# A decode kernel's TensorE program put into one loop of six turns, with its loads re-ordered around it

## Chip, cores, metric

One core of a Trainium2 chip. The metric is the device time of one execution in microseconds, median over runs. Spans and instants are from one profiled execution of each kernel and count from its first instruction.

## The reference, cut to what matters

```python
xn = layernorm(x)                              # x: 2 x 1 x 448
q  = xn @ wq                                   # 448 x 4096: 16 heads of 256
k, v = last 2048 keys of each cache            # 2 x 8 heads x 2048 x 256 each
s  = softmax(q k^T / 16) v @ wo                # wo: 4096 x 448
g  = silu(relu(xn @ w1) @ w2)                  # 448 x 1792, 1792 x 448
out = x + s * g
```

One row per batch: nearly all of the work is reading 44.1 MB of K, V and weights from HBM. The caches are taken in four units u = (batch, half of the heads), each with 4.19 MB of K and 4.19 MB of V.

## The kernel before

A small helper writes one program per engine, with semaphores between them. SP issues all large loads in program order into one queue; PE (the matmul engine) runs the four units as a loop of four turns; DVE (VectorE) transposes K and does the softmax. What the argument needs (cuts marked with `# ...`):

```python
def load_k(u):      # two K buffers: k2 waits for the scores S(0), k3 for S(1)
    d_k[u] = pr.dma(SP, kbuf[u % 2][:, :], kv_src(u, A_k_cache), [st.get(("S", u - 2, NBLK - 1))])

def load_v(u, cuts=(0, NT)):     # v1 waits for PV(0), v2 for PV(1), v3 only for the q matmuls: own buffer
    deps = [None if u == 0 else st["q_mm"] if u == NU - 1 else st["PV", u - 1]]
    # ...

d_wq = [pr.dma(SP, wq_sb[:, 0:FIRST * HC], ...)]     # a part of wq
load_k(0)
d_wq.append(...)                                     # the rest of wq
load_k(1)
load_v(0)
st["w1"] = pr.dma(SP, w1_sb[:, 0:W2_AT], w1_src)
st["w2"] = pr.dma(SP, w2_sb[...], w2_src)
# ...
for blk in range(NBLK):
    do_T(0, blk)          # DVE: transposes of k0
do_q()                    # PE: 28 matmuls; DVE: q_n; PE: replicate; DVE: q_t
turn_q(0)                 # DVE: the masked q for unit 0
turn(0)                   # S(0), softmax
load_k(2)
turn(1)                   # T(1), S(1), PV(0), softmax, then h and F
load_v(1); load_k(3)
turn(2)
load_v(2); load_v(3, (0, 48, 64))
# ... seven parts of wo
turn(3)
# ... ten filler matmuls, PV(3), attend, wo in 9 tiled slots and 23 x 4 narrow matmuls
```

S(u) are the scores of unit u, T(u) the four transposes before it, PV(u) the weighted sum of V. "Attend" turns PV's result into columns for the wo matmuls, which the tile at_z holds. h is relu(xn @ w1), F is h @ w2, g its silu; xr is xn in columns. The "granted clock" is the share of its full clock that PE was given.

## Time and profile before

| | before |
|---|---|
| time, median (range) | 112.78 us (112.55 to 112.97), 4 runs |
| span of the profiled run | 109.8 us (a run of its own, of 111.31 us) |
| share of the span in which the 16 DMA engines are busy | 95% |
| busy share of PE, DVE | 55%, 57% |
| end of S(0), when k2 may be issued | 36.7 us |

### The profile page before, as it was taken

Reading aid. Unit: us, or ns where it says so; the run is one execution under the profiler, and the core shown is the slowest. Engines: PE = TensorE matmul, PEld = TensorE weight load, DVE = VectorE, ACT = ScalarE, POOL = GpSimd, SP = SyncE. Lnnn points to the kernel's source line nnn. Section 1 sums busy time; section 2 is a strip of 40 time slices with the busy share of each in tenths; the row PEclk is TensorE's granted clock in tenths of the full one; section 3 lists DMA queues with packets and bytes.
Section 4 is the critical chain, followed back from the end, with each engine's and each line's share of the span. In section 5 each row is a group of like instructions: output and inputs, shape, how many; then the busy total and the mean of one; then the engine's idle time right before and its main releaser. Section 6 shows DMA issues by size and latency. Waiting matters only on the chain. (4 is left out here: it accounts for less than half of the span.)

```text
span 109.8 us, 1368 instructions
## 1 busy us (share of the span) xinstructions
PE 60.4 (55%) x558; PEld 19.5 (18%) x558; DVE 63.0 (57%) x96; ACT 10.2 (9%) x19; POOL 3.1 (3%) x11
## 2 busy tenths in 40 slices
PE   0001000076599330899755597853039785898993
PEld 0000000020111020000241010112001011534792
DVE  0249109995400459993468999266299926624601
ACT  4990000000000110000200000020000002000000
POOL 7400000000000000000000000000000000000000
PEclk9999999999999995579996569997555899999999
DMA  3998989998899889998899999999999999899950
GB/s 60 502 388 382 549 371 395 439 537 382 382 453 501 382 367 416 411 548 382 382 501 394 406 406 465 441 406 406 465 441 406 444 430 430 361 419 410 402 207 7
DMA packets 3046, 44.15 MB, mean 402 GB/s; under 512 B 354, under 2 KB 612, under 8 KB 1508
## 3 DMA queue, kind: packets, MB, share of 16 engines
q1 hardware_dynamic: 3008, 44.11, 95.0%
q8 instruction: 2, 0.03, 0.1%
q10 hardware_dynamic: 36, 0.01, 0.1%
HBM read 44.11 MB, written 0.00 MB: 402 GB/s over the span
## 5 line engine op out<-in xcount | busy, mean ns | idle before, releaser
L379 DVE STREAM_TRANSPOSE kt<-kbuf 128x2048 f32<-128x2048 f32 x16 | 35.9, 2286 | 7.8 <-DMA kbuf<-in_A_k_cache_dram 7.8
L361 PE MATMUL sbk<-kt,qz 128*8 128x512 bf16 x128 | 31.1, 1073 | 13.6 <-PEq L102 13.5
L401 DVE TENSOR_REDUCE rm<-sbk 128x1 f32<-128x512 f32 x4 | 2.8, 692 | 14.6 <-PE sbk L361 14.6
L361 PE MATMUL obk<-vbuf,xr 128*4 128x512 bf16 x28 | 3.2, 626 | 13.9 <-DMA vbuf<-in_A_wq_dram 13.9
L407 ACT ACTIVATE et<-sbk,bias 128x512 bf16<-128x512 f32 x4 | 2.7, 687 | 81.1 <-DVE bias L405 81.1
L361 PEld LDWEIGHTS sbk<-kt,qz 128*8 128x8 bf16 x128 | 2.6, 87 | 28.9 <-issue 28.7
L361 PE MATMUL pbk<-et,spread 128*128 128x32 bf16 x64 | 2.6, 193 | 7.2 <-PEq L102 7.2
L361 PE MATMUL obk<-vbuf,pt 128*16 128x512 bf16 x96 | 5.8, 381 | 0.0
L361 PE MATMUL mbk<-ident,xg 2*128 2x2 bf16 x7 | 0.3, 163 | 8.5 <-DVE xg L325 8.5
L361 PE MATMUL wbk<-q_n,ident 128*128 128x512 bf16 x15 | 4.1, 395 | 1.4 <-DVE qz L396 1.4
L361 PE MATMUL hbk<-kbuf,at_z 128*8 128x112 bf16 x92 | 4.8, 213 | 0.0
L409 DVE STREAM_TRANSPOSE et<-et 128x512 bf16<-128x512 bf16 x4 | 2.8, 712 | 3.4 <-ACT et L407 3.4
L417 DVE TENSOR_TENSOR pt<-pbk,hmask 128x512 bf16<-128x512 f32 x4 | 2.8, 692 | 3.3 <-PE pbk L361 3.3
L361 PEld LDWEIGHTS hbk<-kbuf,at_z 128*8 128x8 bf16 x92 | 4.6, 87 | 0.1
L361 PEld LDWEIGHTS pbk<-et,spread 128*128 128x128 bf16 x64 | 2.2, 99 | 10.5 <-issue 10.5
L361 PEld LDWEIGHTS obk<-vbuf,pt 128*16 128x16 bf16 x96 | 2.5, 94 | 6.8 <-issue 4.7
L361 PEld LDWEIGHTS obk<-vbuf,xr 128*4 128x4 bf16 x28 | 0.8, 114 | 15.4 <-issue 15.4
L611 DVE TENSOR_TENSOR tmp<-hbk,g_sb 8x112 f32<-8x112 f32 x1 | 0.3, 262 | 4.4 <-PE hbk L361 4.4
L361 PE MATMUL fbk<-wf,h_z 128*2 128x448 bf16 x14 | 1.7, 567 | 1.7 <-DVE h_z L494 1.7
L456 DVE TENSOR_TENSOR at_exp<-mbk,qmask 128x128 bf16<-128x128 f32 x4 | 1.2, 292 | 2.5 <-PE mbk L361 2.5
L361 PE MATMUL obk_last<-vbuf,pt 128*16 128x512 bf16 x32 | 2.3, 380 | 0.0
L444 DVE TENSOR_SCALAR o_sb<-obk,rs 128x512 bf16<-128x512 f32 x3 | 2.2, 731 | 0.0
(80 smaller groups left out, 43.9 us busy)
## 6 DMA issues: line engine op xcount, KB each, us to landing
kbuf<-in_A_k_cache_dram SPq DMA_DIRECT2D x4, 4096.0 KB, 23.4
vbuf<-in_A_v_cache_dram SPq DMA_DIRECT2D x3, 4096.0 KB, 15.8
wf<-in_B_w_dram SPq DMA_DIRECT2D x2, 1568.0 KB, 42.4
vbuf<-in_A_v_cache_dram SPq DMA_DIRECT2D x1, 3072.0 KB, 22.5
vbuf<-in_A_wq_dram SPq DMA_DIRECT2D x1, 2560.0 KB, 20.9
vbuf<-in_A_wq_dram SPq DMA_DIRECT2D x1, 1024.0 KB, 6.1
vbuf<-in_A_v_cache_dram SPq DMA_DIRECT2D x1, 1024.0 KB, 24.4
kbuf<-in_A_wo_dram SPq DMA_DIRECT2D x1, 1008.0 KB, 26.2
```

What stands on the lines that cost most here:

```text
L361: return lambda e: e.matmul(out_ap, lhsT=lhsT, rhs=rhs, start=start, stop=stop, skip_group_check=True, **kw)
L379: st["kt", u, blk] = pr.op(DVE, lambda e: e.transpose(view(dst, 0, [[1, 32 * NT]]), view(src, 32 * blk, [[DH // 2, NT], [1, 32]])), [d_k[u ...
L401: v = pr.op(DVE, lambda e: e.tensor_reduce(out=rm[:, :], in_=sbk[:, :], axis=AX.X, op=ALU.max), [st["S", u, NBLK - 1]])
L407: a = st["exp", u] = pr.op(ACTE, lambda e: e.activation(e_sb, sbk[:, :], ACT.Exp, bias=bias[:, 0:1], accum_out=ssum[:, 0:1]), [v, st.get(( ...
L409: token = pr.op(DVE, lambda e: e.transpose(e_t, e_sb), [a, st.get(("Pt", u - 1))])
L417: st["pt", u] = pr.op(DVE, lambda e: e.tensor_tensor(out=view(pt, 0, [[8, NT], [2, 4], [1, 2]]), in0=view(pbk, 0, [[2, NT], [0, 4], [1, 2] ...
L444: st["osb", u] = pr.op(DVE, lambda e: e.tensor_scalar(out=o_sb[:, :], in0=view(out_bank(u), 0, [[1, 512]]), scalar1=rs[:, u:u + 1], scalar ...
L456: st["at", u] = pr.op(DVE, lambda e: e.tensor_tensor(out=view(at_exp, 0, [[16, 8], [8, 2], [1, 8]]), in0=view(mbk, 136, [[1, 8], [8, 2], [ ...
L611: v_t = pr.op(DVE, lambda e: e.tensor_tensor(out=tmp[:, :], in0=hbk[0:NROW, 0:NCOL], in1=g_sb[:, :], op=ALU.mult), [m_o, v_g])
```

## The change

Its intent is a smaller PE program: one loop of six turns with conditional parts, so that the last PV and both late attends need no code of their own; one V buffer, so that all PVs share code; h and xr by register loops; h computed before the loop, which needs w1 early; F and wo with fewer matmuls; two stores. Behind each of v0 to v2 SP now issues an almost empty transfer ("nil"), so that every PV can wait for two transfers, as PV(3) must for the two parts of v3. The core of the diff:

```diff
-            deps = [None if u == 0 else st["q_mm"] if u == NU - 1 else st["PV", u - 1]]
+            deps = [st["PV", u - 1] if u else None]
...
-        d_wq = [pr.dma(SP, wq_sb[:, 0:FIRST * HC], wq_src[:, 0:FIRST * HC])]
+        d_wq = pr.dma(SP, wq_sb[:, 0:SLOTS * HC], wq_src)
+        st["w1"] = pr.dma(SP, w1_sb[:, 0:W2_AT], w1_src)
         load_k(0)
-        d_wq.append(...)
         load_k(1)
         load_v(0)
-        st["w1"] = ...
-        st["w2"] = ...
...
         def do_H():
-            deps = [st["w1"]]
-            for s in range(SLOTS):
-                for i in range(4):
-                    ... 4 column tiles of 224
+            def body(e, s):
+                for j in range(7):
+                    o = mm(view(hbk, 64 + 4 * j, [[1, 4]]), view(w1_sb, FC * s + j, [[7, 128]]), view(xr, 4 * s, [[1, 4]]), False)(e)
+                return o
+            o = looped(SLOTS, body, [st["w1"]])
...
         for blk in range(NBLK):
             do_T(0, blk)
         do_q()
         turn_q(0)
-        idle_work(1, [st["q"]])
+        do_H()
+        pr.op(PE, None, [st["q"]])
         turn(0)
...
         load_v(2)
-        load_v(3, (0, 48, 64))
+        load_w2()
+        turn(3)
...     (first part of wo, then)
+                load_v(3)
...     (the other parts of wo)
-        idle_loop(5, 2)
-        ... PV(3), attend(2), attend(3) written out, filler matmuls
+        turn(NU)          # attend(2), F, PV(3)
+        turn(NU + 1)      # attend(3)
```

Attend moved from between the transposes to the head of each turn; F is 14 matmuls one after the other instead of four tiles side by side; wo is 16 tiled slots and 16 x 2 matmuls of 224 columns.

## The prediction

The "start-up ramp" is in the trace of the kernel before: 83, 181 and 385 GB/s in the second, third and fourth microsecond, 582 in the fifth. The doubling for strided reading was my estimate (0.08 us a pair from the 0.04 of the trace); the 0.5 us a turn and the 2 us restart of the rivals and the 1 us outside the span were suppositions, shown by no trace. That low PE use brings a low clock was not shown: the trace gives the clock of 0.57 and PE's busy time, 3.42 of 10 us, side by side from 74 to 84 us; the cold tail in the range was an estimate from that.

> **What bounds the kernel now.** I read the page first (engine shares, the slices, the DMA queue), then the waits of the DMA-issuing queue on SP, then the timeline. The page:
>
> ```profile
> DMA  3998989998899889998899999999999999899950
> ...
> q1 hardware_dynamic: 3008, 44.11, 95.0%
> ...
> HBM read 44.11 MB, written 0.00 MB: 402 GB/s over the span
> ```
>
> The sixteen DMA engines are busy from the second slice to the last but two; no compute engine passes 57%. The kernel is a stream of 44.1 MB with work hung beneath it. The timeline shows when SP issued the transfers, all in one queue:
>
> ```profile
> 5.10 1.09 SPq L42 DMA_DIRECT2D wf<-in_B_w_dram  x2
> 36.73 0.55 SPq L42 DMA_DIRECT2D kbuf<-in_A_k_cache_dram  x1
> 54.34 0.54 SPq L42 DMA_DIRECT2D vbuf<-in_A_v_cache_dram  x1
> 54.92 0.60 SPq L42 DMA_DIRECT2D kbuf<-in_A_k_cache_dram  x1
> 72.85 1.83 SPq L42 DMA_DIRECT2D vbuf<-in_A_v_cache_dram  x3
> ```
>
> and the waits of SP before them:
>
> ```profile
> SPq L42 <- PE obk L361: 34.4, 2, 17.3
> SPq L42 <- PE sbk L361: 30.5, 1, 30.5
> ```
>
> SP waits long, for PE to free K and V buffers, yet the DMA never pauses: what it issued earlier is still draining. So the quantity that decides is the lead, the time between the issue of a transfer and the moment the queue ahead of it would run dry. To get it I need landings. The waiting engines give them:
>
> ```profile
> 16.61 8.89 DVE L379 STREAM_TRANSPOSE kt<-kbuf 128x2048 f32<-128x2048 f32 x4 [5.30 <-DMA kbuf<-in_A_k_cache_dram]
> 22.78 3.16 PE L361 MATMUL obk<-vbuf,xr 128*4 128x512 bf16 x28 [13.91 <-DMA vbuf<-in_A_wq_dram]
> 25.99 0.69 DVE L478 TENSOR_SCALAR q_n<-obk 128x512 bf16<-128x512 f32 x1 [0.49 <-PE obk L361]
> 29.24 7.45 PE L361 MATMUL sbk<-kt,qz 128*8 128x512 bf16 x32
> 41.54 8.88 DVE L379 STREAM_TRANSPOSE kt<-kbuf 128x2048 f32<-128x2048 f32 x4
> 52.37 1.92 PE L361 MATMUL obk<-vbuf,pt 128*16 128x512 bf16 x32
> 59.51 2.31 DVE L379 STREAM_TRANSPOSE kt<-kbuf 128x2048 f32<-128x2048 f32 x1 [0.28 <-DMA kbuf<-in_A_k_cache_dram]
> 78.95 4.51 DVE L379 STREAM_TRANSPOSE kt<-kbuf 128x2048 f32<-128x2048 f32 x2 [2.27 <-DMA kbuf<-in_A_k_cache_dram]
> ```
>
> Cumulated in order of issue, k0 ends 5.24 MB (landed 16.6), wq 7.86 MB (22.75), k2 23.65 MB (59.5), k3 32.04 MB (78.95), the first wo part 41.45 MB (100.9, where the chain of waits has its 26.22 us DMA piece end). One line fits all five: landing = 4.45 us + MB / 0.4297 MB per us. A K or V block of 4.19 MB takes 9.76 us. The first issue was at 0.74, so a transfer into an empty queue lands 3.7 us later than its bytes alone account for. The last byte is due at 4.45 + 44.11/0.4297 = 107.1, and the span ends 2.7 us later. Leads before: k2 issued at 36.7 with the queue filled to about 53; v1 and k3 at 54.3 with it filled to 59.5; v2 at 72.85 with it filled to 79. All exceed 3.7 us.
>
> [...] 30.5 us of waiting lies on SP, and five landings lie on one line in order of issue. [...] In the trace the instruction queue moved 2 packets (0.1% of DMA time), and at turn starts PE begins about 0.15 us after the transpose it needs (59.51 + 2.31 = 61.82, matmul 61.97): there is no fetch stall to win back.
>
> **The change, part by part.**
>
> *Order of loads.* Now wq (3.67 MB), w1 (1.61), k0, k1, v0, then the wait for S(0) before k2; w2 and the first wo part moved behind v2. The bytes are the same. From the line: wq 13.0, w1 16.7, k0 26.5 (was 16.6), k1 36.2, v0 46.0. Nothing is queued behind v0; before, w1 and w2 gave 7.5 us more.
>
> *First scores.* VectorE runs in program order and the four transposes of k0 stand ahead of the q chain, though wq is there at 13. Transposes 26.5 + 8.9 = 35.4. The q chain (q_n, a replicating matmul, transpose, two masks) took 2.65 us from q_n's start to 28.64: now until 38.1. h is computed on PE before S(0), behind the replicating matmul (36.8): 49 pairs with full 128-column weights read at a stride of 7. The spread matmuls (128-column weights, contiguous) cost 0.65/16 = 0.04 us a pair; for strided reading I take twice that, about 4 us with seven loop turns, so until 40.8. This is an estimate. S(0) takes 7.45 as before: ends 48.4 instead of 36.7. The queue ran dry at 46.0. k2 lands at 48.4 + 3.7 + 9.8 = 61.9 instead of 55.8: 6.1 us of bubble.
>
> *v1.* From the end of S(0) to the end of PV(0) was 54.3 - 36.7 = 17.6 us of softmax, transposes, S(1), PV(0). k2 keeps the DMA busy only 13.5 us of that. v1 is issued at 66.0, lands at 79.5 instead of 71.6: 7.9 us. k3 follows at 89.2.
>
> *Turns 2 and 3.* Attend (turn and spread) moved ahead of the transposes, one round trip more between PE and VectorE, about 1.1 us less the 0.5 that it cost among the transposes. S(1) ends 64.3. Softmax, scale and masks 5.7, attend 1.1, transposes 8.9, last scores 2.1: S(2) ends 82.1, PV(1) 83.9. v2 then has a lead of 5.3 us: no bubble, lands 99.0. T(3) waits for k3 at 89.2, S(3) ends 100.2, PV(2) 102.0.
>
> *One V buffer.* Before, v3 had its own buffer, free since the q matmuls. Now it waits for PV(2): issued 102.0, plus 3.7 is 105.7, against the queue's end (w2 and nine wo slots behind v2) at 105.1: 0.6 us. v3 lands 115.5, the other 2.64 MB of wo at 121.6. Sum of bubbles 6.1 + 7.9 + 0.6 = 14.6 us on 107.1.
>
> *Tail.* F now runs untiled in turn 4 after the attend (about 106.5): 14 x 448 columns; at the half clock granted there before (0.50 around 59 to 61 us) the tiled groups of four took 0.37 us, so 14 x 0.37 = 5.2. exp and add 1.2; reciprocal (0.84 us for 112 columns against 0.16 for one: 6 ns a column) 3 us for 448; two products 0.8: g at 116.7, just ahead of or level with the last scale. PV(3)'s last quarter, scale, attend and spread: at_z at 119. Sixteen tiled slots 1.5, copy 0.6, fold 0.4: 121.5. The last sixteen slots in two column groups 2 to 2.5: 124. The final two VectorE operations and the store took 1.8 from the last matmul: span 125.8. Warm-up matmuls went away; [...] this trace shows 0.57 in a stretch with PE idle (74 to 84 us). That is in the upper half of the range. Two stores instead of one go out from two queues side by side: 0. The three nil transfers carry no bytes that count.
>
> Time less span was 112.77 - 109.8 = 3.0: about 128.5. As h may be quicker than 4 us and 3.7 us contains a start-up ramp, I put 128.
>
> **Rivals.**
> *Bytes alone decide* (a stream stays full): same bytes, end at 107, within 1%. For it: DMA 95% busy. Against it: k2's wait for S(0), which needs k0 and the transposes; only with S(0) over by about 42 would the stream hold, and 26.5 + 8.9 + 2.7 + 7.45 = 45.5 even with h free. Time 112 to 113.
> *Fewer PE instructions win*: no fetch, cheaper tail. At most the 2.7 us after the last byte and perhaps 1 us outside the span: 110 to 112.
> *Small bubbles*: h costs nothing and a restart costs 2 us, not 3.7. S(0) 45.6, bubbles 1.6 + 6.1, then the chain of turns: 120 to 122.
> *Fetch or loop stalls*: six turns with nested conditions, each on the path since VectorE now sets the pace; 0.5 us each gives 3 us more: 131 to 132.
>
> **Range and chances.** Low end from small bubbles, high end from stalls with a cold tail: 121 to 133. The order of loads and waits is read from the program, so slower by over 2% is 0.94; within 2% 0.04; faster 0.02.
>
> **What would show it.** DMA slices with holes near 46 to 50 and 62 to 68 us; k0's transposes starting near 26.5; S(0) ending near 48; SP's issue of k2 near 48 and of v1 near 66; DMA share near 83%; the last wo landing near 121. It is wrong if S(0) ends before 42, or if v1 is issued before k2 has landed.

## The result, and the profile after

The changed kernel took 132.28 us (131.31 to 133.29, 4 runs; one of them, more than 1.5% above the fastest, counts as slow and is left out of the ratio), against 112.78 us: ratio 1.170, 95% interval 1.163 to 1.178. Ratios here are the mean time of one kernel's fast runs over that of the other's fast runs of the same rounds, so not quite the ratio of the medians. The profiled run is the longest of the three fast ones: its span is 131.1 us at a mean granted clock of 0.74, the others have 129.8 and 130.5 us at 0.88 and 0.87.

The page of the changed kernel, the lines that answer to the first fence of the prediction:

```profile
DMA  5999999998998200489700989989989999989900
...
q1 hardware_dynamic: 2964, 44.11, 79.8%
...
HBM read 44.11 MB, written 0.00 MB: 336 GB/s over the span
```

The same bytes, now with two gaps of zeros: a slice is 3.3 us, so they lie at about 46 to 52 and 66 to 72 us. Read stretch by stretch, the DMA moved nothing from 44 to 54 us and from 65 to 72 us. The instruction queue, 2 packets before, is gone from this page. That the smaller program is the cause is not shown: the run with the q chain first, below, has as many instructions and shows two packets (0.02 MB and less than 0.01 MB).

SP's timeline and its waits in the changed kernel (start, duration, what was issued; for the waits total, times, longest):

```profile
3.63 0.60 SPq L45 DMA_DIRECT2D nil<-in_A_x_dram  x1
53.10 0.54 SPq L45 DMA_DIRECT2D kbuf<-in_A_k_cache_dram  x1
70.67 0.54 SPq L45 DMA_DIRECT2D vbuf<-in_A_v_cache_dram  x1
71.88 0.54 SPq L45 DMA_DIRECT2D kbuf<-in_A_k_cache_dram  x1
88.06 0.53 SPq L45 DMA_DIRECT2D vbuf<-in_A_v_cache_dram  x1
105.64 1.20 SPq L45 DMA_DIRECT2D vbuf<-in_A_v_cache_dram  x2
```

```profile
SPq L45 <- PE sbk L359: 48.9, 1, 48.9
SPq L45 <- PE obk L359: 48.1, 3, 17.0
```

Between 4.2 and 53.1 us SP issued nothing: 48.9 us in one wait for S(0), 18 more than before, and what had been issued ran out at 44, 9 us too early. Where S(0) was, the timeline shows this, after one line of the kernel before, where h stood behind PV(0):

```profile
56.43 0.84 PE L361 MATMUL hbk<-wf,xr 128*4 128x224 bf16 x28
```

```profile
25.26 8.89 DVE L384 STREAM_TRANSPOSE kt<-kbuf 128x2048 f32<-128x2048 f32 x4 [11.87 <-DMA kbuf<-in_A_k_cache_dram]
34.08 0.65 DVE L474 TENSOR_SCALAR q_n<-obk 128x512 bf16<-128x512 f32 x1
35.19 0.93 PE L359 MATMUL hbk<-xr,wf 128*128 x7
...
43.50 0.99 PE L359 MATMUL hbk<-xr,wf 128*128 x7 [0.41 <-issue]
...
45.69 7.37 PE L359 MATMUL sbk<-kt,qz 128*8 128x512 bf16 x32 [1.20 <-PEq L105]
```

k0 arrives at 25.3 instead of 16.6 (wq and w1 are ahead of it), DVE, idle for 11.87 us until then, transposes it and only then, at 34.1, comes to q_n, though the q matmuls had ended at 16. Then h: seven turns of the register loop, each 0.99 us of matmuls and 0.41 us of idle PE, 9.3 us in all; then 1.2 us in PE's sequencer until the first matmul of S(0). In the kernel before, h took 0.84 us. S(0) ends at 53.1 instead of 36.7.

And the end of the changed kernel:

```profile
110.33 5.20 PE L359 MATMUL fbk<-wf,h_z 128*2 128x448 bf16 x14 [0.23 <-issue]
116.55 2.94 DVE L511 RECIPROCAL tmp<-q_t 2x448 f32<-2x448 f32 x1
118.72 0.61 PE L359 MATMUL obk<-vbuf,pt 128*16 128x512 bf16 x8 [1.01 <-PEq L105]
119.52 0.77 DVE L513 TENSOR_TENSOR g_sb<-fbk,tmp 2x224 f32<-2x224 f32 x2
120.33 0.75 DVE L441 TENSOR_SCALAR o_sb<-obk,rs 128x512 bf16<-128x512 f32 x1
122.60 1.66 PE L359 MATMUL tbk<-kbuf,at_z 128*2 128x448 bf16 x16 [0.49 <-DVE at_z L463]
125.70 3.20 PE L359 MATMUL hbk<-kbuf,at_z 128*2 128x224 bf16 x32
```

F, 1.66 us long in the kernel before, is over at 115.5, its exp, reciprocal and products keep DVE until 120.3; the last quarter of PV(3) had ended at 119.3, so the last scale waits 1.0 us for g. Then the wo matmuls run on until 128.9, at a granted clock of 0.50 to 0.57, while the DMA has been silent since 125: the tail is PE's, not the stream's.

### The profile page after: what moved, and what is told of

Read it like the earlier page. It is cut to its first block, busy times and chain, and to the rows that moved or that the text cites. A ratio compares the mean times of both kernels' runs of the same rounds, so it can differ in the third digit from the quotient of the medians.

```text
span 131.1 us, 1372 instructions
## 1 busy us (share of the span) xinstructions
PE 65.9 (50%) x499; PEld 22.4 (17%) x499; DVE 64.8 (49%) x94; ACT 10.9 (8%) x20; POOL 3.5 (3%) x13
## 2 busy tenths in 40 slices
DMA packets 2980, 44.11 MB, mean 336 GB/s; under 512 B 418, under 2 KB 676, under 8 KB 1572
## 3 DMA queue, kind: packets, MB, share of 16 engines
q1 hardware_dynamic: 2964, 44.11, 79.8%
HBM read 44.11 MB, written 0.00 MB: 336 GB/s over the span
## 5 line engine op out<-in xcount | busy, mean ns | idle before, releaser
L359 PE MATMUL pbk<-q_n,qrep 128*128 128x512 bf16 x1 | 0.6, 610 | 18.7 <-DVE q_n L474 18.7
L359 PE MATMUL obk<-vbuf,pt 128*16 128x512 bf16 x128 | 7.9, 381 | 1.7 <-PEq L105 1.7
L359 PE MATMUL hbk<-xr,wf 128*128 x49 | 6.9, 208 | 2.4 <-issue 2.4
L359 PE MATMUL mbk<-ident,xg 2*128 2x2 bf16 x7 | 1.2, 178 | 11.3 <-DVE par L328 8.5
L359 PEld LDWEIGHTS hbk<-xr,wf 128*128 x49 | 6.2, 131 | 3.3 <-issue 3.0
L359 PE MATMUL fbk<-wf,h_z 128*2 128x448 bf16 x14 | 5.2, 561 | 0.2 <-issue 0.2
L359 PEld LDWEIGHTS obk<-vbuf,pt 128*16 128x16 bf16 x128 | 3.5, 93 | 9.8 <-issue 7.5
L359 PE MATMUL mbk<-fold,o_sb 128*128 128x8 bf16 x16 | 1.0, 167 | 6.1 <-PEq L105 6.1
L359 PE MATMUL hbk<-kbuf,at_z 128*2 128x224 bf16 x32 | 3.2, 391 | 0.0
```

The costliest lines, as they stand in the source:

```text
L359: return lambda e: e.matmul(out_ap, lhsT=lhsT, rhs=rhs, start=start, stop=stop, skip_group_check=True, **kw)
```

## The experiments

Eleven runs, all correct. They were made on several chips, and the kernel before took 111.4 to 112.3 us on them. The changed kernel's time hangs on engines rather than on the HBM, so beside the ratios I compare instants and spans of the profiles. Line numbers differ by a few between kernels.

### The start

**h written out.**

```diff
-            o = looped(SLOTS, body, [st["w1"]])
+            for s in range(SLOTS):
+                for j in range(7):
+                    o = pr.op(PE, mm(view(hbk, 64 + 4 * j, [[1, 4]]), view(w1_sb, FC * s + j, [[7, 128]]),
+                                     view(xr, 4 * s, [[1, 4]]), False), [st["w1"]])
```

> The changed kernel with the 49 matmuls of h written out with constant addresses instead of the register loop; everything else as it is. In the changed kernel h took 9.3 us, of it about 0.4 us of idle PE before each of the seven turns. Theory A (the end of S(0) carries one to one through to the end): h falls to about 6.5 us, S(0) ends about 2.5 to 3 us earlier, time about 129.5. Rival R1 (the size of the PE program and fetches decide): 84 more PE instructions, time the same or longer, 132 to 134.

Measured: 125.0 us, ratio 1.108 (1.097 to 1.119), span 122.8. More than expected. Its timeline:

```profile
35.33 2.75 PE L359 MATMUL hbk<-xr,wf 128*128 128x4 bf16 x49
...
38.27 7.40 PE L359 MATMUL sbk<-kt,qz 128*8 128x512 bf16 x32 [0.19 <-PEq L105]
```

The 49 matmuls take 2.75 us (0.056 us a pair with its weight load) instead of 9.3, and the wait before S(0) is 0.19 instead of 1.20. So the register loop was not idle time between turns alone: each pair in it also took 0.99/7 = 0.14 us. What in the loop makes a pair slower was not measured. A slower clock is not the reason: in the changed kernel the loop ran at a granted clock of 0.50, in the next run at 1.00, with the same 0.99 and 0.41 us. One instruction packet is on the page (0.02 MB; the next run, with as many instructions as the changed kernel, has one of that size too) and cost nothing visible. k2 is issued at 45.7 instead of 53.1.

**The q chain ahead of k0's transposes on DVE.**

```diff
-        for blk in range(NBLK):
-            do_T(0, blk)
         do_q()
         turn_q(0)
+        for blk in range(NBLK):
+            do_T(0, blk)
         do_H()
```

> The changed kernel with the q chain ahead of the transposes of k0 in VectorE's program order; nothing else. wq lands at 13 us, so q and h should be over at about 27 us while k0 is still arriving, and S(0) ends right behind the transposes, near 36.5 us instead of 53.1. Theory A: the first hole in the DMA stream goes, the chain of turns moves forward by 16 us; one hole of about 1.5 us is left before v3: time 116 to 118. Rival R2 (single V buffer and the tail are what cost, the start is hidden by later waits): 129 to 132. Rival R1 (loop and branch costs of the six turns): 129 to 132.

Measured: 114.7 us, ratio 1.030 (1.020 to 1.041), span 113.4: theory A, a little better than its 116. h now runs while k0 is still on its way:

```profile
25.53 8.89 DVE L384 STREAM_TRANSPOSE kt<-kbuf 128x2048 f32<-128x2048 f32 x4 [6.71 <-DMA kbuf<-in_A_k_cache_dram]
25.63 0.99 PE L359 MATMUL hbk<-xr,wf 128*128 x7 [0.41 <-issue]
...
36.58 0.54 SPq L45 DMA_DIRECT2D kbuf<-in_A_k_cache_dram  x1
```

Moving two lines gives back 17.7 us of span. The slow loop is still there and costs nothing, because it is over before the first transpose is. The order of the loads is still there as well: what costs is that DVE's order had been left as it was when k0 came first. The hole that is left lies before v1 (DMA share 0.71 and 246 GB/s from 52 to 56 us) and not, as expected, before v3.

**w1 behind k0.**

```diff
-        st["w1"] = pr.dma(SP, w1_sb[:, 0:W2_AT], w1_src)
         load_k(0)
+        st["w1"] = pr.dma(SP, w1_sb[:, 0:W2_AT], w1_src)
```

> The changed kernel with w1 queued behind k0 instead of ahead of it: k0 lands 3.7 us earlier (1.61 MB at 0.43 MB per us), w1 then still lands before h needs it. Theory A: S(0) ends 3.7 us earlier and the time is 3.7 us less, about 128.6. If the transfers are only re-ordered within a stream that sets the end by its bytes, the time stays at 132.3.

Measured: 128.78 us, ratio 1.152 (1.141 to 1.162), span 127.5 instead of 131.1: 3.6 us, as theory A has it.

The four kernels together show how the start carries through:

| kernel | k2 issued at | span | difference |
|---|---|---|---|
| changed | 53.10 | 131.1 | 78.0 |
| w1 behind k0 | 49.50 | 127.5 | 78.0 |
| h written out | 45.70 | 122.8 | 77.1 |
| q chain first | 36.58 | 113.4 | 76.8 |

Over 16.5 us the end follows S(0) almost one to one. From k2's issue to the last at_z copy it is 69.1, 69.1, 68.4 and 69.2 us. Most of the missing microsecond in the last row is in the last wo matmuls: 2.6 us instead of 3.9 for the group with the fold, which took 3.6 with h written out.

### Holes, or the chain?

**w2 early.** This run tells apart two readings of the same trace: the prediction had added up the holes in the DMA stream.

```diff
+        st["w2"] = pr.dma(SP, w2_sb[...], w2_src)     # right behind load_v(0)
...
-        load_w2()                                     # behind load_v(2)
```

> The changed kernel with w2 queued right behind v0 again, as the kernel before had it, instead of behind v2: 1.61 MB, 3.7 us of traffic, go into the first hole. Theory A1 (as the prediction added it up: the sum of the holes in the DMA stream sets the end): the time falls by 3.7 us to 128.6. Theory A2 (the chain of turns from the end of S(0) to PV(2) sets when v3 is issued, and everything after hangs on that): the hole only moves to before v3, the time stays within 1 us of 132.3.

Measured: 132.69 us, ratio 1.187 (1.177 to 1.197), span 130.7: theory A2. Stretches of this run's trace (window, length, busy time and count of PE, PEld, DVE, ACT, POOL, granted clock, DMA share, GB/s):

```profile
104.00:106.00 2.00, 2.00 (x36) 0.71 (x28) 1.23 (x4) 0.00 (x0) 0.00 (x0) 1.00 0.58 242
106.00:107.00 1.00, 0.34 (x8) 0.00 (x0) 0.16 (x2) 0.78 (x2) 0.00 (x0) 1.00 0.00 0
```

Traffic that was moved into the first hole left a new one just before v3, which SP issued at 106.4, when PV(2) was over. From k2's issue to v3's it is 52.5 us here and in the changed kernel. (The two spans by themselves would say less: k2 was issued 0.8 us later in this run, and its last wo group was 1.2 us shorter.) Here the holes are not what costs; they are the shadow of the chain S(0), T, S, PV, turn after turn. In one place chain and stream are level: in the changed kernel k3 landed at 92.9, just as T(3) began. That wait can be 0.2 us at most, since T(2) followed its own at_z copy only 0.2 us sooner.

**A second V buffer for v3**, alone and together with w2 early.

```diff
-            deps = [st["PV", u - 1] if u else None]
+            deps = [None if u == 0 else st["q_mm"] if u == NU - 1 else st["PV", u - 1]]
+            vb = vbuf[u // (NU - 1)]
...                                       (PV(3) gets a block of its own in the loop)
```

> The changed kernel with a V buffer of its own for v3 (wq's buffer, free since the q matmuls), nothing else. v3 then is issued without waiting for PV(2). In the changed kernel w2 and the first wo part filled the queue almost up to v3's issue, and behind v3 the last scale waits for g on VectorE until 120.3 anyway. Theory A (the late start, not the single buffer, costs): ratio to before 1.16 to 1.175, as the changed kernel's 1.170. If the single buffer is the cause: below 1.12.

Measured: 132.85 us, ratio 1.183 (1.177 to 1.188). No gain (a little above the range that I gave; the kernel before was quicker on this chip than beside the changed kernel, and the span, 131.3, is the changed kernel's 131.1). v3 was issued at 90.5 instead of 105.6, but behind w2 and wo it landed at 119.0, as before.

> The changed kernel with both: the second V buffer for v3 and w2 behind v0. Each alone should do nothing, since v3 waits either for PV(2) or for w2 and wo ahead of it in the queue; both together let v3 land about 3 us earlier, near 115.5. Theory A: the gain is cut to 1 us or less, because F and g, which hang on the chain of turns, then hold the last scale until 120: ratio 1.155 to 1.17. If the DMA stream alone sets the end: 3 us less, 1.14.

Measured: 132.54 us, ratio 1.178 (1.172 to 1.183), span 131.4: no gain, and again a little above the range given. Here v3 had landed by 115 and PV(3) was over at 117.7, 1.7 us earlier than in the changed kernel, and the last scale still ran at 120.6, because DVE was busy with F's reciprocal and products until then. So behind PV(2) two paths of nearly the same length lead to the last scale, one by v3 and one by F and g; shortening the first does nothing.

### Parts of the change in the kernel before

**The order of the first loads alone.**

```diff
-        d_wq = [first part]; load_k(0); d_wq.append(rest); load_k(1); load_v(0); w1; w2
+        d_wq = [all of wq]; w1; load_k(0); load_k(1); load_v(0); w2
```

> The kernel before with only the order of the first loads changed: wq whole, w1, k0, k1, v0, w2 (before: a quarter of wq, k0, the rest of wq, k1, v0, w1, w2). No other edit, so h is still computed in turn 1. Theory A: k0 lands near 25.3 instead of 16.6, S(0) ends near 45.4; k2 still has 4 us of lead because w2 is queued behind v0, but v1 is issued at 63 when the queue ran dry at 59.5: one hole of some 7 us, ratio to before about 1.06. If bytes alone decide: 1.00.

Measured: 118.93 us, ratio 1.061 (1.050 to 1.072); k2 issued at 46.2, v1 at 64.7, no traffic from 60 to 66 us. As expected: no hole at k2, since w2 still stood behind v0, and one at v1.

**One V buffer alone**, with the first wo part ahead of v3.

```diff
-            deps = [None if u == 0 else st["q_mm"] if u == NU - 1 else st["PV", u - 1]]
+            deps = [None if u == 0 else st["PV", u - 1]]
...         (vbuf[0] for all units; load_v(3) behind the first part of wo)
```

> The kernel before with one V buffer for all four turns and the first wo part issued ahead of v3, as the change has it; nothing else. v3 then waits for PV(2), which ended near 92.3, while the queue is filled to 91.7. With a restart of 3.3 us as the changed kernel's v3 showed it: a hole of about 4 us, ratio 1.035. If the single buffer costs nothing: 1.00. If it is the main cost of the change: over 1.08.

Measured: 118.99 us, ratio 1.064 (1.055 to 1.073). The hole is of the expected size: SP issued v3 at 92.1, 8 GB/s or less from 90 to 93 us. (The "restart of 3.3 us" was a misreading: in the changed kernel the stream did not pause at v3, with 419 to 475 GB/s from 105 to 109 us. From an empty queue, as here, the first three quarters of v3 landed 10.0 us after their issue, 2.7 us more than their 3.15 MB take at the prediction's rate.) The other 3 us I had missed; they are in the tail:

```profile
102.11 1.88 PE L361 MATMUL obk_last<-vbuf,pt 128*16 128x512 bf16 x16 [3.79 <-DMA vbuf<-in_A_v_cache_dram]
...
110.99 4.69 PE L361 MATMUL hbk<-kbuf,at_z 128*8 128x112 bf16 x92
```

With a wo part sent ahead, only 2.64 MB follow v3, and the stream ends at about 111, before PV(3), attend and 92 narrow matmuls are through; PV(3)'s first half took 1.88 us instead of 1.04, the granted clock being 0.65 and 0.50 here (100 to 104 and 104 to 108 us) and 1.00 in the kernel before. In that kernel, its DMA busy for 95% of the span, the single buffer, with a wo part ahead of v3, did cost 6.4%; in the changed kernel a second buffer gained nothing (1.183 with it, 1.170 without), because the wait was covered.

### The tail, and everything put back

**Tail of the run with the q chain first.**

```diff
+        do_g()                 # the two products of g behind the last at_z copy
+                idle_work(4)   # behind PV(3)
+        idle_work(3)           # while the sums are copied
```

> The run with the q chain first (ratio 1.030), and in its tail the two products for g moved behind the last at_z copy on VectorE, four filler matmuls behind the last PV and three while the sums are copied. In that run the last scale waited 1.2 us for g, and the wo matmuls ran at half clock (tbk 1.65 us for 16, hbk 1.9). Theory: the tail behind v3 shortens by 0.9 us (g) and 0.8 to 1.5 us (clock), ratio about 1.010. If the last transfer already sets the end: 1.03 as before.

Measured: 113.77 us, ratio 1.019 (1.010 to 1.029), span 111.3 against 113.4. The 16 tiled wo matmuls took 0.93 us instead of 1.66, at a granted clock of 0.98 to 1.00 instead of 0.65 and 0.50 (106 to 107 and 107 to 108 us; 0.50 and 0.65 in the next two microseconds, under the others). The 2.1 us of span are what was expected, 1.0 us of it before the last at_z copy and 1.1 behind; the three edits were not tried apart. The ratio shows less of it (1.030 to 1.019), and the two intervals overlap.

**All waits of SP with their lead again**: in addition w2 behind v0, the second V buffer, F at the end of turn 3.

> The previous one and further w2 queued behind v0, a second V buffer for v3 [...], and the FFN matmuls at the end of turn 3. All waits of the issuing queue then have their lead again. Theory A: the DMA stream has no hole, the last byte lands near 107 as in the kernel before, and the time is that of the kernel before within 1 per cent (0.99 to 1.01), with the loop of six turns, the register loops and two stores still in it. Rival R1 (loops and branches cost by themselves): it stays above 1.015.

Measured: 111.47 us against 111.38, ratio 0.999 (0.993 to 1.004), span 110.0. The page of this run:

```profile
DMA  6798999999899999998999999999999899999940
```

No hole. The loop of six turns, both register loops, the wider wo and two stores are all in it, and the time is that of the kernel before. The three edits of this step were not tried apart either.

**v3 ahead of all wo parts** in that version.

```diff
+        load_v(3)
         d_wo, j0 = {}, 0
...
-            if j0 == 0:
-                load_v(3)
```

> The version with everything put back (ratio 0.999) with v3 issued ahead of all wo parts, as the kernel before has it, instead of behind the first. v3 should land 2.4 us earlier (98.6 instead of 101.0), and PE then waits for the last wo parts, which land near 107 in either order: 0.3 to 0.7 us less, ratio 0.993 to 0.997. If the last bytes already set the end in that version: 0.999.

Measured: 112.11 us against 112.30, ratio 0.997 (0.992 to 1.001). At_z is ready 0.8 us earlier, and PE then waits for the last two wo parts (0.17 and 0.20 us before its last matmuls); the span stays at 110.0. No version beat the kernel before by an amount clear of noise.

## Why the prediction was right

| step | predicted | measured |
|---|---|---|
| k0 lands | 26.5 | 25.3 |
| DVE comes to q_n | 35.4 | 34.1 |
| h on PE, and the way into the loop | 4.0 + 0.1 | 9.3 + 1.2 |
| S(0) ends, k2 issued | 48.4 | 53.1 |
| from there to v1's issue | 17.6 | 17.6 |
| k2 and v1, each into an empty queue: landing after issue | 13.5 | 12.5, 12.5 |
| from S(0)'s end to v3's issue | 53.6 | 52.6 |
| from v3's issue to its last quarter in use | 13.5 | 13.1 |
| F; reciprocal | 5.2; 3 | 5.20; 2.94 |
| from S(0)'s end to the last matmul | 75.6 | 75.9 |
| DMA share | 83% | 79.8% |

The direction, the mechanism and the place were right: loads ahead of k0, VectorE's program order, h before S(0), SP's in-order wait, no lead left, and the time within the range, close to its upper end. Neither sign of being wrong came: S(0) did not end before 42, and v1 was issued at 70.7, after k2 had landed at 65.6.

**The mis-sized term is h.** "about 4 us with seven loop turns" measured 9.3 us, plus 1.2 us until S(0)'s first matmul (0.19 with h written out, so most of that wait is the register loop's too). The weights read at a stride were not the reason: written out, the 49 pairs took 0.056 us each, less than the 0.08 I had allowed. The loop was. How far the order of the loads goes without h is seen in the kernel before with that order alone: S(0) ended at 46.2 there, 9.4 us later than before, of the 16.4 us in all. The term for h is 6.4 us too little, less 1.6 us by which h could begin earlier (35.2 instead of 36.8, since k0 landed earlier) and 0.1 us in S(0). With the way from S(0) to the last matmul right to 0.3 us and 0.4 us more after it, the span comes out 5.3 us longer than the predicted 125.8. In the time 1.5 us of that is taken back: I had put time less span at 3.0 us, from a median and a profiled run that do not belong together; in the profiled runs it is 1.5 in both kernels.

**Two readings were off without effect.** In "k2 issued at 36.7 with the queue filled to about 53" the prediction's own line gives 49.7 for the 19.46 MB queued by then; the lead is 13 us and not 16, still ample. And a restart was put at 3.7 us beyond the bytes: k2 and v1 landed 12.5 us after their issue, 2.7 us more than the 9.76 us of a block, their first traffic 1.3 us after it (54.4 and 72.0 us). The chain did not wait for either of them; it met the stream only at k3, where the prediction too had the two level (88.9 and 89.2).

**The adding of bubbles was the wrong way to the right sum.** "Sum of bubbles 6.1 + 7.9 + 0.6 = 14.6 us" treats holes as costs. The run with w2 early shows that a hole can be filled without gain. The sum came out because the last term tied v3 to PV(2), so it followed the chain anyway; that much was luck. The "0.6 us" for one V buffer was right in effect: a second buffer changed nothing.

**g against the last scale.** "just ahead of or level with the last scale": it was 1.0 us behind it. It mattered more than its size, since it takes away what an earlier v3 would give.

**The rivals.** Bytes alone: the same 44.11 MB took 1.17 times as long. Small bubbles: the restart was indeed shorter than 3.7 us (2.7), but h was far from free. Fetch and loop stalls by themselves: the version with everything put back keeps six turns and conditions at a ratio of 0.999, so the branches cost nothing where they are covered; the two register loops are the exception in size (h's left PE idle for 0.41 us a turn; the seven turns for xr, one matmul each, came 0.62 to 0.69 us apart, where written out all seven took 0.34 us), and h's cost only where S(0) had to wait for it. Fewer PE instructions win: the instruction packets went from 2 to between none and two, with nothing to show for it. The cold tail, named as the upper half of the range: its granted clock was 0.50 to 0.57 from 122 to 129 us, 1.00 in the last wo matmuls of the kernel before; fillers and the moved products gave 2.1 us of span.

How the 21.3 us of span divide among S(0)'s 16.4 us and the rest is shown; how the 6.5 us that h loses to being looped (9.3 less 2.75) divide between the address in the register, the loop's own instructions and the branch stays open.

## What to carry to other kernels

In this kernel, its DMA busy for 95% of the span, the number to guard was the lead of the issuing queue: how long what is already queued lasts beyond the moment when the next buffer is freed. In these runs, whatever came before the first release (the order of the first loads, the program order of the engine that prepares them, an unrelated product squeezed in ahead) was paid almost one to one once the lead was used up (span less k2's issue stayed at 76.8 to 78.0 us), and h's 9.3 us cost nothing with the q chain first, where they were over before S(0) could start. When the loads were re-ordered, the engine that prepares them should have been re-ordered with them: that was 17.7 us of span. A hole in the transfer row was a symptom in the changed kernel (with w2 moved into it the span was 130.7 us against 131.1), and a cost with one V buffer in the kernel before (118.99 us against 111.38): move traffic into one and see whether the end moves before treating it as the cause.
